# Casting v block by block, slicing W_in, and scores by tanh and pow, in a cross-covariance attention + GELU MLP kernel

One NeuronCore of one Trainium2 chip. The metric is the device time of one execution in microseconds (us), median over runs; lower is better.

## The reference

```python
def _attn_ref(q, k, v, tau):                 # each (4, 6080, 256) float32, tau = 1
    qn = q / (np.linalg.norm(q, axis=1, keepdims=True) + 1e-06)
    kn = k / (np.linalg.norm(k, axis=1, keepdims=True) + 1e-06)
    s = kn.transpose(0, 2, 1) @ qn / tau     # 256 x 256 per batch
    s = s - s.max(-1, keepdims=True)
    a = np.exp(s)
    a /= a.sum(-1, keepdims=True) + 1e-09
    return (v @ a).astype(np.float32)

# x is the attention's output, its four batches one below the other; c (line cut) is sqrt(2 / pi)
def _moe_ref(x, w_in, w_out):                # (24320, 256), (256, 2048), (2048, 256)
    h = x @ w_in
    g = 0.5 * h * (1.0 + np.tanh(c * (h + 0.044715 * h * h * h)))
    return (g @ w_out).astype(np.float32)
```

## The kernel before

Attention is folded into the first MLP product: per batch the kernel computes the Gram matrix of q and k and the sums of squares, then the scores, then `AW` = softmax times W_in. After that each block of 512 tokens (12 blocks per batch, 48 in all) takes a first product with `AW`, a gelu on ScalarE, and a second product with W_out. v must arrive transposed, so it is cast to bf16 through DRAM by a DMA from GpSimd and read back by transposing DMAs from SyncE. While one batch's blocks run, the next batch's q and k are loaded, and its Gram rows go between the block's matmuls. The parts that matter (cuts are marked by dots):

```python
qkp = ctx.enter_context(tc.tile_pool(name="qkp", bufs=6))
...
def cast_v(b, t0, t1):
    nc.gpsimd.dma_start(out=v_bf[b][t0:t1, :], in_=v[b, t0:t1, :])

def load_vt(n):                       # block n of v, transposed
    ...
    for cc in range(2):
        nc.sync.dma_start_transpose(
            out=vT[:, cc, :cols], in_=v_bf[b][t0 : t0 + cols, cc * 128 : cc * 128 + 128])
...
def scores(b):
    ss = SS[b]                        # sums of squares, the same in every partition
    nc.scalar.activation(lnk, ss[:, 256:512], AF.Ln, bias=eps)
    # ... VectorE takes q's sums off the diagonal into qq ...
    nc.scalar.activation(rk, lnk, AF.Exp, scale=-0.5)
    nc.scalar.activation(lnq, qq, AF.Ln, bias=eps)
    nc.scalar.activation(rq, lnq, AF.Exp, scale=-0.5, bias=log_it)
    # ... S = G * rk on VectorE ...
    for jc in range(2):
        nc.scalar.activation(eT[:, jc, :], S[:, jc, :], AF.Exp, scale=rq[:, jc : jc + 1])
    nc.scalar.preload_act_table(AF.Gelu_apprx_tanh)
...
        VC = 1024
        for c in range(nch):
            load_qk(0, c)
            if c == 3:
                cast_v(0, 0, VC)      # blocks 0 and 1
                load_vt(0)
            squares(0, c)             # (cut: on the last chunk a GpSimd memset of its padding)
            for i in range(len(rows_of(0, c))):
                gram_row(0, c, i)
                ss_row(0, c, i)
        nc.gpsimd.dma_start(out=win_bf, in_=moe_w_in.rearrange("(c p) d -> p c d", p=128))
        nc.gpsimd.dma_start(out=wout_bf, in_=moe_w_out.rearrange("(t p) d -> p t d", p=128))
        cast_v(0, VC, N)
        load_vt(1)
        scores(0)
        ...
        for n in range(NN + 1):       # 48 blocks; blk = n % 12, nxt = next batch
            for p in range(PAIRS):    # 8 steps
                if p == 0: load_vt(n + 2)
                mm1(n, p)             # first product and gelu
                mm2(n - 1, p)         # second product of the block before
                if p == 7: store(n - 1)
                if p == 0 and 1 <= blk <= 6: load_qk(nxt, blk - 1)
                if p == 0 and blk == 7:      cast_v(nxt, 0, N)
                # blk 2 to 7: Gram rows of chunk blk - 2 of the next batch
                # blk 8: ss_total, scores, row_sums;  blk 9: aw_part
```

## Time and profile before

| | before |
|---|---|
| median of 4 runs | 824.0 us (821.0 to 825.3) |
| span of the profiled run | 821.1 us |
| PE busy, mean granted clock | 92%, 0.969 |
| block 0's first product starts | 50.6 us |
| block 0's start to the end of block 3 | 81.55 us |
| blocks 8 to 12 (scores of batch 1) | 83.23 us |
| blocks 20 to 24 (batch 2), 32 to 36 (batch 3) | 81.76 us, 82.50 us |

"Block n" in these rows means pass n of the loop above; a pass ends where the store in it is issued, which is the output of block n - 1. The last three rows are lengths of stretches cut at those points. Between these stretches PE is 100% busy. The lines themselves are in the prediction. In them and in all lines below, PE is TensorE, DVE is VectorE, ACT is ScalarE, POOL is GpSimd and SP is SyncE; a row of a timeline has its start and length in us, and `[x <-y]` says that the engine was idle for x us before it and what ended that. A transfer has landed when all its data is in place.

### The profile page before, as it was taken

What the parts mean: (1) busy time and instruction counts of PE and PEld (TensorE: products, weight loads), DVE (VectorE), ACT (ScalarE), POOL (GpSimd) and SP (SyncE); (2) the same over time, 40 slices, a digit from 0 to 9 for tenths busy, and PEclk for the clock granted to TensorE, in tenths of its full rate; (3) what the DMA queues carried; (4) which work ended last, traced back from release to release, by engine and by line L of the source; (5) the groups of instructions that cost most, each with busy time, mean ns of one, the idle gap of its engine ahead of it and who ended that gap; (6) DMA issues with size and microseconds to landing.
All of it is one profiled execution on the core that took longest, in us unless ns stands there. A gap on an engine that the chain in (4) does not pass through costs nothing.

```text
span 821.1 us, 11523 instructions
## 1 busy us (share of the span) xinstructions
PE 756.7 (92%) x5126; PEld 505.5 (62%) x5126; DVE 177.8 (22%) x246; ACT 473.8 (58%) x470; POOL 38.4 (5%) x75
## 2 busy tenths in 40 slices
PE   5776679999799999999799999999799999999997
PEld 2434447776457667676466666767466666666666
DVE  1121115333111133433121133343121111111111
ACT  3273346566655567565765565756756555555552
POOL 4121000201000000011000000000000000000000
PEclk9998689999899999999899999999899999999999
DMA  9999971499962213199931211212112121212111
GB/s 177 181 210 206 216 153 40 91 218 128 100 151 68 46 40 78 39 207 162 201 79 39 75 40 39 77 39 39 39 38 77 40 74 40 77 40 71 44 52 49
DMA packets 87698, 77.57 MB, mean 94 GB/s; under 512 B 53584, under 2 KB 80720, under 8 KB 87120
## 3 DMA queue, kind: packets, MB, share of 16 engines
q0 software_dynamic: 10784, 39.46, 26.8%
q1 hardware_dynamic: 76864, 37.37, 20.6%
q8 instruction: 40, 0.66, 0.3%
q14 instruction: 10, 0.08, 0.0%
HBM read 78.91 MB, written 37.36 MB: 142 GB/s over the span
## 4 chain that ended last, share of the span: by engine, by line
PE 79%; DMA 16%; ACT 2%; SPq 1%; issue 0%; POOL 0%; DVE 0%; DVEq 0%; POOLq 0%
PE yp L263 37%; PE hp L243 36%; DMA vT<-vbf 9%; PE G L153 4%; DMA vbf<-in_v_dram 3%; DMA kt<-in_k_dram 2%; SPq L99 1%; DMA qt<-in_q_dram 1%; PE ps L219 1%; ACT g L247 1%; PE ss L166 0%; ACT L198 0%; ACT L189 0%; ACT L187 0%; ACT L179 0%
## 5 line engine op out<-in xcount | busy, mean ns | idle before, releaser
L247 ACT ACTIVATE g<-hp 128x1024 bf16<-128x1024 f32 (+1 forms) x384 | 388.9, 1015 | 298.5 <-PE hp L243 296.8
L243 PE MATMUL hp<-vT,aw 128*128 128x512 bf16 (+1 forms) x1536 | 398.4, 383 | 39.7 <-DMA vT<-vbf 21.4
L263 PE MATMUL yp<-wout_bf,g 128*128 128x256 bf16 (+1 forms) x3072 | 402.0, 275 | 0.0
L263 PEld LDWEIGHTS <-g 128*128 128x128 bf16 (+1 forms) x3072 | 303.3, 99 | 118.6 <-issue 7.3
L243 PEld LDWEIGHTS <-aw 128*128 128x128 bf16 x1536 | 150.6, 99 | 153.1 <-issue 44.5
L269 DVE COPY ysb<-yp 128x512 f32<-128x512 f32 x92 | 63.6, 691 | 481.2 <-PE yp L263 481.2
L153 PE MATMUL G<-kt,qt 128*128 128x256 bf16 (+1 forms) x384 | 76.6, 282 | 12.9 <-DMA kt<-in_k_dram 12.9
L120 ACT ACTIVATE sq<-qt 128x2048 bf16<-128x2048 bf16 (+3 forms) x25 | 45.0, 1801 | 26.0 <-DMA qt<-in_q_dram 13.4
L153 PEld LDWEIGHTS <-qt 128*128 128x128 bf16 (+1 forms) x384 | 38.5, 101 | 25.5 <-issue 10.2
L121 DVE TENSOR_TENSOR sq<-kt 128x2048 bf16<-128x2048 bf16 (+3 forms) x25 | 28.9, 1154 | 30.7 <-DMA kt<-in_k_dram 28.0
L166 PE MATMUL ss<-sq,ones_bf 128*128 128x512 bf16 (+1 forms) x48 | 21.0, 437 | 2.6 <-DVE sq L121 2.6
L133 DVE TENSOR_TENSOR a<-a 128x1024 f32<-128x1024 bf16 x18 | 22.0, 1225 | 0.6
L131 DVE TENSOR_TENSOR a<-sq 128x2048 bf16<-128x2048 bf16 x18 | 21.9, 1215 | 0.0
L219 PE MATMUL ps<-win_bf,eT 128*128 128x512 bf16 x64 | 19.8, 405 | 2.2 <-DMA win_bf<-in_moe_w_in_dram 2.2
L226 DVE TENSOR_SCALAR aw<-ps,rs 128x512 bf16<-128x512 f32 x16 | 12.0, 751 | 39.7 <-PE ps L219 39.7
L119 POOL MEMSET sq<- 128x512 bf16 x4 | 2.1, 525 | 383.1 <-DVE a L131 371.5
L79 POOL DMA_DIRECT2D qt<-in_q_dram x25 | 13.9, 554 | 80.6 <-ACT g L247 59.0
L224 ACT ACTIVATE aw<-ps,rs 128x512 bf16<-128x512 f32 x16 | 11.0, 688 | 7.4 <-PE ps L219 7.4
L79 POOL DMA_DIRECT2D kt<-in_k_dram x25 | 13.8, 553 | 25.2 <-DMA vbf<-in_v_dram 11.4
L142 DVE TENSOR_TENSOR acc<-acc,a 128x512 f32<-128x512 f32 x15 | 10.4, 692 | 0.5
L141 DVE TENSOR_TENSOR a<-a 128x512 f32<-128x512 f32 x15 | 10.4, 692 | 0.5
L219 PEld LDWEIGHTS <-eT 128*128 128x128 bf16 x64 | 6.5, 102 | 5.6 <-DMA win_bf<-in_moe_w_in_dram 2.3
(40 smaller groups left out, 67.4 us busy)
## 6 DMA issues: line engine op xcount, KB each, us to landing
out_dram<-ysb SPq DMA_DIRECT2D x44, 512.0 KB, 3.3
qt<-in_q_dram POOLq DMA_DIRECT2D x20, 512.0 KB, 14.5
kt<-in_k_dram POOLq DMA_DIRECT2D x20, 512.0 KB, 16.9
vbf<-in_v_dram POOLq DMA_DIRECT2D x3, 3040.0 KB, 28.8
vbf<-in_v_dram POOLq DMA_DIRECT2D x1, 2528.0 KB, 23.5
vT<-vbf SPq DMA_TRANSPOSE x96, 3.6
out_dram<-ysb SPq DMA_DIRECT2D x4, 384.0 KB, 2.6
qt<-in_q_dram POOLq DMA_DIRECT2D x3, 448.0 KB, 8.0
```

Source lines behind the costliest of these rows:

```text
L79: nc.gpsimd.dma_start(out=t[:, 0:n, :], in_=src[b, 0 : R * 128, :].rearrange("(p r) c -> p r c", r=R)[:, r0 : r0 + n, :])
L120: nc.scalar.activation(sq[:, 0:n, 0:256], qt[:, 0:n, :], AF.Square)
L121: nc.vector.tensor_mul(sq[:, 0:n, 256:512], kt[:, 0:n, :], kt[:, 0:n, :])
L131: nc.vector.tensor_add(a1, sq[:, 0:4, :], sq[:, 4:8, :])
L133: nc.vector.tensor_add(a2, a1[:, 0:2, :], a1[:, 2:4, :])
L153: nc.tensor.matmul(G[b][:, jc, :], lhsT=qt[:np_, r, jc * 128 : jc * 128 + 128], rhs=kt[:np_, r, :], start=first and jc == 0, stop=last and ...
L166: nc.tensor.matmul(SS[b], lhsT=ones_bf[:np_, :], rhs=SQ[b, c][:np_, r, :], start=first, stop=last)
L219: nc.tensor.matmul(ps, lhsT=ET[b][:, jc, ic * 128 : ic * 128 + 128], rhs=win_bf[:, jc, fs * 512 : fs * 512 + 512], start=jc == 0, stop=jc ...
L243: nc.tensor.matmul(hp[:, u, :cols], lhsT=AW[b][:, cc, fc * 128 : fc * 128 + 128], rhs=vt_tiles[n][:, cc, :cols], start=cc == 0, stop=cc == 1)
L247: nc.scalar.activation(GS[n][:, 2 * p : 2 * p + 2, :cols], hp[:, :, :cols], AF.Gelu_apprx_tanh)
L263: nc.tensor.matmul(yp[:r, s % 2, :], lhsT=GS[n][:, fc, s * 128 : s * 128 + r], rhs=wout_bf[:, fc, :], start=fc == 0, stop=fc == FC - 1)
L269: nc.vector.tensor_copy(ysb[:, s - 1 : s + 1, :], yp)
```

## The change

Three intents: (1) v is cast in pieces of 512 tokens, three blocks ahead of use, through a pool of four buffers, so that a block no longer waits for a cast of several MB; one transpose of 256 columns replaces two of 128. (2) W_in comes in four column slices right behind batch 0's q and k; batch 0's row sums run one chunk behind its Gram rows; the padding memset moves from GpSimd to VectorE. (3) Batches 1 to 3 get their scores without Ln and Exp: norms by a pow of 0.5 on GpSimd, and exp(x) as (1 + tanh(x/2)) / (1 - tanh(x/2)). One eviction of batch 0's `AW` also moves from ScalarE to VectorE (not shown).

```diff
-    dram = ctx.enter_context(tc.tile_pool(name="dram", bufs=1, space=bass.MemoryType.DRAM))
+    dram = ctx.enter_context(tc.tile_pool(name="dram", bufs=4, space=bass.MemoryType.DRAM))
...
-        sizes = [8, 8, 8, 8, 8, 4, 3] if b == 0 else [8, 8, 8, 8, 8, 7]
+        sizes = [8, 8, 8, 8, 8, 5, 2] if b == 0 else [8, 8, 8, 8, 8, 7]
...
-    def cast_v(b, t0, t1):
-        nc.gpsimd.dma_start(out=v_bf[b][t0:t1, :], in_=v[b, t0:t1, :])
+    def cast_v(n):
+        ...
+        vb = dram.tile([BLK, C], BF16, tag="vb", name=f"vb{n}")
+        nc.gpsimd.dma_start(out=vb[:cols, :], in_=v[b, t0 : t0 + cols, :])
+        v_bf[n] = vb
...
-        for cc in range(2):
-            nc.sync.dma_start_transpose(
-                out=vT[:, cc, :cols], in_=v_bf[b][t0 : t0 + cols, cc * 128 : cc * 128 + 128])
+        nc.sync.dma_start_transpose(out=vT[:, :, :cols], in_=v_bf.pop(n)[:cols, :])
...
-            nc.gpsimd.memset(sq[:, n, :], 0.0)
+            nc.vector.memset(sq[REM:, n, :], 0.0)
...
+    def norms(b):
+        ... # VectorE: q's sums off the diagonal to sv[:, 256:258], k's copied to sv[:, 0:256]
+        rt = smx.tile([128, 258], FP32, tag="rt")
+        nc.gpsimd.tensor_tensor(rt, sv, halves, op=ALU.pow)
+    def scores_a(b):
+        ... # VectorE: rt + 1e-6, reciprocal, S = G * rr
+    def scores_b(b):
+        ... # ScalarE: th = tanh(S * rh), twice
+    def scores_c(b):
+        ... # VectorE: eT = (1 + th) / (1 - th)
...
-            if c == 3:
-                cast_v(0, 0, VC)
+            if c == 1:
+                cast_v(0)
                 load_vt(0)
             squares(0, c)
             for i in range(len(rows_of(0, c))):
                 gram_row(0, c, i)
-                ss_row(0, c, i)
+            if c: ... # ss_row of chunk c - 1; those of the last chunk after the loop
-        nc.gpsimd.dma_start(out=win_bf, in_=...)
+        for fs in range(4):
+            nc.gpsimd.dma_start(out=win_bf[:, :, fs * 512 : fs * 512 + 512], in_=wi[...])
+        cast_v(1)
+        load_vt(1)
         nc.gpsimd.dma_start(out=wout_bf, in_=...)
-        cast_v(0, VC, N)
-        load_vt(1)
+        cast_v(2)
...
                         load_vt(n + 2)
+                    if p == 0 and n + 3 < NN:
+                        cast_v(n + 3)
                     mm1(n, p)
...
-                    if p == 0 and blk == ncn + 1:
-                        cast_v(nxt, 0, N)
...
                     if blk == 8:
                         if p == 2:
                             ss_total(nxt)
-                            scores(nxt)
+                            norms(nxt)
                         if p == 6:
+                            scores_a(nxt)
+                    if blk == 9:
+                        if p == 1: scores_b(nxt)
+                        if p == 2: scores_c(nxt)
+                        if p == 7:
                             row_sums(nxt)
-                    if blk == 9:
+                    if blk == 10:
                         aw_part(nxt, p // 2, p % 2, "act" if p % 2 else "dve")
```

## The prediction

> **What bounds the kernel now.** I read the page first, then the busy times by stretch, the waits of the matmul engine, the timeline around each idle gap, and the time to landing of the transposes.
>
> The page's 40 slices (20.5 us each, in tenths busy) come first.
>
> ```profile
> PE   5776679999799999999799999999799999999997
> ...
> PEclk9998689999899999999899999999899999999999
> DMA  9999971499962213199931211212112121212111
> ```
>
> The matmul row is full but for slices 0 to 5 and for single slices (10, 19, 28); the clock dips at the same places. DMA is full exactly in the early hole. So there are two kinds of loss: one where transfers are the bound, and three short ones, one per later batch. Stretches cut at the output stores show them (columns: stretch, length, busy us and instructions of each engine, granted clock, DMA share, GB/s).
>
> ```profile
> 0.00:50.60 50.60, 30.34 (x156) 16.63 (x157) 10.50 (x21) 17.40 (x17) 16.01 (x33) 0.93 1.01 181
> 50.60:132.15 81.55, 60.75 (x365) 37.29 (x364) 15.10 (x19) 37.77 (x37) 4.80 (x9) 0.85 0.89 176
> 132.15:194.71 62.56, 62.56 (x449) 43.57 (x448) 25.06 (x29) 39.60 (x37) 5.85 (x11) 1.00 0.70 135
> 194.71:218.20 23.49, 17.58 (x106) 10.73 (x105) 2.73 (x9) 16.89 (x19) 2.66 (x5) 0.85 1.47 85
> ...
> 385.82:409.33 23.51, 17.60 (x106) 10.68 (x105) 2.73 (x9) 16.88 (x19) 2.67 (x5) 0.85 1.11 205
> 409.33:575.46 166.13, 166.13 (x1168) 113.78 (x1167) 46.87 (x57) 102.23 (x99) 0.53 (x1) 1.00 0.22 53
> 575.46:599.71 24.25, 18.34 (x106) 11.01 (x105) 2.72 (x9) 16.88 (x19) 0.00 (x0) 0.86 0.12 33
> ```
>
> Where PE is 100% busy nothing can be won: 62.56 us are four token blocks with Gram work, 15.64 us each, and the plain block takes 13.9 us (spacing of the last stores). A pair of steps (4 matmuls of 512 columns, 8 of 256) starts every 1.74 us, 2.35 columns per ns. The losses are in the rest.
>
> Early hole, waits of PE from 40 to 135 us, and PE in it:
>
> ```profile
> PE hp L243 <- DMA vT<-vbf: 20.4, 3, 9.3
> ...
> 79.38 0.61 PE L243 MATMUL hp<-vT,aw 128*128 128x512 bf16 x1 [5.27 <-DMA vT<-vbf]
> 89.33 1.44 PE L243 MATMUL hp<-vT,aw 128*128 128x512 bf16 x3 [9.34 <-DMA vT<-vbf]
> 113.52 1.44 PE L243 MATMUL hp<-vT,aw 128*128 128x512 bf16 x3 [5.75 <-DMA vT<-vbf]
> ```
>
> Blocks 2 and 3 wait for the transposed v. The transposes were late twice over: the 5 MB cast of v landed at 64.5 us, and behind it next batch's q and k filled the queue. Time to landing of a transpose, first in 60 to 120 us, then after 260 us:
>
> ```profile
> DMA to landing us min/median/max: 3.3/18.9/37.8
> ...
> DMA to landing us min/median/max: 2.6/3.4/24.6
> ```
>
> Scores hole, ACT from 390 us:
>
> ```profile
> 390.91 1.28 ACT L179 ACT_TABLE_LOAD   x1
> 392.20 0.47 ACT L179 ACTIVATE lnk<-ss,eps 128x256 f32<-128x256 f32 x1
> 392.70 1.28 ACT L187 ACT_TABLE_LOAD   x1
> ...
> 398.58 1.28 ACT L198 ACT_TABLE_LOAD   x1
> ```
>
> Five loads of 1.28 us lie between two gelus (390.89 to 399.87); PE then shows a 5.91 us gap and four matmuls taking 1.86 in place of 1.03 us.
>
> **What the Trainium skill says.** "ScalarE: Activation LUTs", section What ACT_TABLE_LOAD costs, gives about 1283 ns for a load plus about 1380 ns of drain. The trace agrees on the load (1.28 us, five of them), but shows no drain of that length beside it: 8.98 us are 6.4 us of loads, 2.4 us of activations (0.47, 0.42, 0.29, 0.29 and 0.91) and small gaps. "TensorE: Matmul & The Clock Gate", Part 1, says that an idle window of about 3.4 us halves the clock; the trace agrees (granted clock 0.85 over each scores block, that is half speed for some 7 of 23.5 us). "DMA: Bandwidth & Descriptors", Queues, rings and completion order, says each engine alternates between queues packet by packet, so a transpose beside a full software queue waits for a load packet at each turn; 18.9 against 3.4 us fits. "GPSIMD Engine Reference", section 3.1, gives some 2.6 cycles per element for a two-input add and nothing for pow; no row of this trace has GpSimd arithmetic of that form, so pow is the term I cannot size.
>
> **Part 1: the start, up to the first gelu block.** Now: the last k part is in at about 37.7 us (issued 24.39, 13.3 us to landing); the last chunk's squares wait for PE to free a buffer until 38.6; sums end at 42.1; scores of batch 0 end at 44.8; then PE waits 2.2 us for W_in, whose issue sat 11.58 us behind a GpSimd memset, to 39.14; block 0 starts at 50.6. The change moves the memset to DVE, so W_in queues straight behind k, and its first slice (512 KB read, about 1.2 us at the 428 GB/s of reads that 214 GB/s written in bf16 means) is in by 40 us: that wait goes. 512 rows fewer of v go ahead of k: 1.2 us. Gram rows no longer queue behind sums that need squares, and the 3.6 us gap at 28.7 us, with the half clock after it, should shrink: another 1 to 2 us. Sum: block 0 starts at about 46, 4.6 us earlier.
>
> **Part 2: the early hole.** Ideal from block 0 on is 10.3 us (block 0 now, paced by its gelus) + 13.9 + 2 x 15.64 = 55.5 us up to the end of block 3; now it is 132.15 - 50.6 = 81.55 us. So 26.0 us are waits and half-clock restarts. In the new kernel v comes in 256 KB pieces (bf16), and each cast must wait until an older buffer has been transposed; q and k of the next batch are queued between the casts, so the queue can't run 10 MB ahead. What stays: behind k come W_in (1 MB), v block 1, W_out (1 MB), v blocks 2, 3 and 4, and one q/k chunk (1 MB): 4.2 MB or 19.6 us at 214 GB/s from about 36.5 us, so to 56 us, with transposes beside it to 59. Block 1 needs its v at 46 + 10.3 = 56.3 us, its cast lands at about 45, and its transposes share the queue with this backlog. I charge a stall of 2.5 us with the restart. Block 2's v (needed at 70 us) has the queue mostly to itself. Gain: 23.5 us.
>
> **Part 3: scores of batches 1 to 3.** The scores blocks take 23.49, 23.51 and 24.25 us. Without the hole such a block is 13.9 + 0.86 (two fp32 matmuls, 390.54 to 391.40) + 0.2 (last Gram row) = 15.0 us, so 8.5 + 8.5 + 9.2 = 26.2 us are lost. New on ACT: two tanh of 128x256 at about 0.46 us, 0.9 us; a gelu takes 1.02 of each 1.74 us and two PSUM buffers cover the slip, so nothing on the path if no table is loaded. New on DVE: some 5 us over ten steps of 1.74 us, on an engine 22% busy. New on GpSimd: one pow of 128x258. From the sums (end of step 2) to tanh (step 1 of the next block) are seven steps, 12.2 us; DVE work ahead and behind takes about 3.5 us. A pow up to about 9 us is hidden. I charge 1 us for all three. Gain: 25.2 us. The W_in product for the next batch moves a block later, at the same cost.
>
> **Part 4: the rest.** Batch 1's v in one 3 MB cast delayed one block at 236 us by 1.1 us and made that block 15.82 instead of 14.33 us: 1.5 us gained. The tail is untouched.
>
> **Sum.** 4.6 + 23.5 + 25.2 + 1.5 = 54.8 us; 822.8 - 54.8 = 768. Check from below: of the 90 us that PE's span has over its columns (1.72 million at 2.35 per ns, 731 us), the first load, block 0's gelus and the last store remain.
>
> **Rivals.** (a) Pow is slow. For: GpSimd is the slowest for such work, and DVE waits in order behind it, with output evictions queued after. Against: someone left four steps between norms and their use, as if it had been measured. At 20 us some 11 us per batch come back: 800. (b) The transpose wait stays: HWDGE still meets a full software queue in 45 to 60 us, and GpSimd in program order holds q and k back behind a cast that waits for a buffer. For: 18.9 us median beside loads. Against: blocks 1 and 2 have two blocks' lead, after which there is 1.25 MB (6 us of queue) per 15.6 us block. A full transpose delay at blocks 1 and 2 gives 778. (c) Part 1 is worth nothing, because k lands no earlier with transposes of block 0 now beside it: 773. (d) All hidden, no stall at block 1: 762.
>
> **Range and chances.** Parts 2 and 3 are holes seen in the trace, removed at the cause; both would have to fail to stay within 2% (above 806). (d) gives the low end, (b) with (c) or a pow of some 13 us the high end: 757 to 785. Faster 0.96, same 0.03, slower 0.01.
>
> **What would show it.** No wait of PE on the transposes in 60 to 135 us, and block 3 ending near 104 us (Part 2); block 0's first gelu near 46 us (Part 1); no table load after about 45 us, scores blocks of about 15 us, full clock there (Part 3). DVE waiting on pow for over 3 us, or PE on gelu near each batch's eighth block, would prove rival (a); PE waiting on transposed v at blocks 1 to 3, rival (b). The prediction is wrong if pow takes over 12 us, if tanh makes a table load, or if the single transpose of 256 columns is much slower than the two of 128.

## The result, and the profile after

The changed kernel takes **913.4 us** (4 runs, 912.2 to 914.6) against 824.0 us. The ratio is 1.1091 (95% interval 1.1053 to 1.1128): slower by 11%, where I had said 768 us and faster. A ratio here is the mean time of one kernel's fast runs over that of the other's fast runs of the same rounds, so it is not quite the ratio of the medians quoted.

The page's slices (22.8 us each, tenths busy), to be laid beside those of before:

```profile
PE   4657999992388999999147899999905999999997
...
POOL 3412000039720000004962000000595000000000
PEclk9988999997598999999669899999966999999999
DMA  9999521210599121211069913122107321212201
```

The early hole is still there (slices 2 and 3, counted from 0), and each single-slice hole of before is now two to three slices wide. POOL, nearly idle before, is full in or just ahead of each. DMA has a peak right after each POOL peak. One group explains POOL:

```profile
L217 POOL TENSOR_TENSOR rt<-sv,halves 128x258 f32<-128x258 f32 x3 | 125.0, 41653 | 395.3 <-DVE sv L215 395.3
```

The pow takes 41.65 us each time. The chain of waits hands it on; here are VectorE, ScalarE and PE behind the first one, each from its own timeline:

```profile
237.92 0.29 DVE L223 TENSOR_SCALAR rt<-rt 128x258 f32<-128x258 f32 x1 [40.20 <-POOL rt L217]
```

```profile
240.58 0.91 ACT L236 ACTIVATE th<-S,rh 128x256 f32<-128x256 f32 x2 [32.98 <-DVE S L229]
```

```profile
242.44 1.86 PE L292 MATMUL hp<-vT,aw 128*128 128x512 bf16 x4 [31.56 <-ACT g L296]
277.79 1.67 PE L292 MATMUL hp<-vT,aw 128*128 128x448 bf16 x4 [8.57 <-DMA vT<-vb]
```

VectorE waits 40.2 us for pow, ScalarE's tanh 33.0 us for VectorE, and PE 31.6 us for the gelu queued behind the tanh. A second gap follows 35 us later, on transposed v. What lies between is the GpSimd queue (start, length, instruction, idle before it):

```profile
87.31 0.49 POOL L93 DMA_DIRECT2D vb<-in_v_dram  x1 [2.39 <-DMA qt<-in_q_dram]
196.22 41.66 POOL L217 TENSOR_TENSOR rt<-sv,halves 128x258 f32<-128x258 f32 x1 [108.42 <-DVE sv L215]
237.86 2.48 POOL L93 DMA_DIRECT2D vb<-in_v_dram  x5
240.33 0.56 POOL L79 DMA_DIRECT2D qt<-in_q_dram  x1
```

For 108 us GpSimd issues nothing, because the pow at the head of its queue waits for its input; then it computes 41.7 us; then everything queued behind goes out at once.

The waits of PE over the whole run, and the stretches (before: 83.23, 81.76 and 82.50 us for the three with scores):

```profile
PE hp L292 <- ACT g L296: 94.9, 4, 31.6
PE hp L292 <- DMA vT<-vb: 36.4, 4, 13.8
```

```profile
49.20:126.95 77.75, 58.73 (x365) 36.76 (x364) 15.05 (x19) 37.62 (x37) 8.96 (x17) 0.89 0.77 141
126.95:189.51 62.56, 62.56 (x449) 43.58 (x448) 25.41 (x30) 39.61 (x37) 0.00 (x0) 1.00 0.19 51
189.51:307.34 117.83, 77.70 (x504) 50.09 (x503) 17.77 (x29) 43.53 (x46) 55.30 (x27) 0.84 0.54 113
...
415.23:532.96 117.73, 77.16 (x504) 49.90 (x503) 17.77 (x29) 43.53 (x46) 55.28 (x27) 0.84 0.54 113
...
640.85:747.92 107.07, 75.52 (x504) 49.41 (x503) 17.77 (x29) 43.53 (x46) 47.75 (x13) 0.86 0.30 66
```

The books close. Block 0 starts 1.4 us earlier (49.2), blocks 0 to 3 take 3.8 us less, the three scores stretches take 34.6, 36.0 and 24.6 us more: together +90.0 us, and the spans differ by 911.2 - 821.1 = 90.1 us. Batch 3 is cheaper by 10.7 us than batches 1 and 2: there is no batch 4 whose q and k could come in a burst. (That the burst is the reason is shown by e5 and e8 below.)

### The profile page after: what moved, and what is told of

The parts are those of the page before. It is cut to its first block, busy times and chain, and to the rows that moved or that the text cites. A ratio compares the mean times of both kernels' runs of the same rounds, so it can differ in the third digit from the quotient of the medians.

```text
span 911.2 us, 11507 instructions
## 1 busy us (share of the span) xinstructions
PE 756.7 (83%) x5126; PEld 506.4 (56%) x5126; DVE 200.3 (22%) x273; ACT 448.9 (49%) x442; POOL 185.4 (20%) x120
## 4 chain that ended last, share of the span: by engine, by line
PE 66%; DMA 17%; POOL 14%; DVE 1%; ACT 1%; issue 0%; DVEq 0%; POOLq 0%
PE yp L312 32%; PE hp L292 30%; POOL rt L217 14%; DMA vT<-vb 12%; DMA qt<-in_q_dram 4%; PE G L156 3%; DMA wout_bf<-in_moe_w_out_dram 2%; DVE rr L224 1%; PE ps L268 0%; ACT th L236 0%; PE ss L174 0%; ACT g L296 0%; POOL qt L79 0%; POOL kt L79 0%; DVE sv L215 0%
## 5 line engine op out<-in xcount | busy, mean ns | idle before, releaser
L217 POOL TENSOR_TENSOR rt<-sv,halves 128x258 f32<-128x258 f32 x3 | 125.0, 41653 | 395.3 <-DVE sv L215 395.3
L156 PE MATMUL G<-kt,qt 128*128 128x256 bf16 (+1 forms) x384 | 71.6, 290 | 16.1 <-DMA kt<-in_k_dram 16.1
L236 ACT ACTIVATE th<-S,rh 128x256 f32<-128x256 f32 x6 | 2.7, 500 | 98.9 <-DVE S L229 98.9
L93 POOL DMA_DIRECT2D vb<-in_v_dram x48 | 24.4, 511 | 33.4 <-DMA qt<-in_q_dram 26.2
L169 PE MATMUL ss<-sq,ones_bf 128*128 128x512 bf16 (+1 forms) x48 | 11.7, 386 | 0.0
```

Source lines behind the costliest of these rows:

```text
L93: nc.gpsimd.dma_start(out=vb[:cols, :], in_=v[b, t0 : t0 + cols, :])
L156: nc.tensor.matmul(G[b][:, jc, :], lhsT=qt[:np_, r, jc * 128 : jc * 128 + 128], rhs=kt[:np_, r, :], start=first and jc == 0, stop=last and ...
L217: nc.gpsimd.tensor_tensor(rt, sv, halves, op=ALU.pow)
```

## The experiments

Twelve kernels ran, in three sets of four; all gave correct results. "Before" is the old kernel, run in the same rounds (medians 821.6, 822.4 and 821.8 us). My theory A was: pow's duration, plus a burst of loads queued behind it, is the whole loss.

### e1: the change with the old scores

```diff
-                            norms(nxt)          # and scores_a, _b, _c; aw_part in block 10
+                            scores(nxt)         # aw_part in block 9
```

> The changed kernel with the old scores (Ln, Exp, table loads) for batches 1 to 3; everything else of the change stays. Theory A (the pow of 41.65 us on GpSimd, and the loads queued behind it, are the whole loss): 816 to 819 us, since the changed kernel's block 3 ended 5.2 us earlier than before (126.95 against 132.15) and the second v wait of the old kernel goes (1.5 us). Rival B (the casts of v by block, the W_in slices or the single transpose cost time after block 3 too): above 830 us.

Measured 817.6 us (ratio 0.9982, 0.9921 to 1.0042). Theory A holds and rival B falls: everything but the scores is no slower than before, and no faster worth naming. So the loss is in part 3, and parts 1 and 2 had gained next to nothing.

### e2: the kernel before with the new scores only

```diff
-                            scores(nxt)
+                            norms(nxt)          # and scores_a, _b, _c; aw_part in block 10
```

> The kernel before with nothing but the new scores (pow, tanh) put in. Theory A: slower by three times 33.9 less 8.5 us (stall and half clock with pow, less the old table loads), +76 us, so 899 us, and up to 20 us more if the loads that wait behind the pow collide with transposes as in the changed kernel. Rival B: well below 870 us.

Measured 919.2 us (ratio 1.1205, 1.1162 to 1.1248), within the bounds of A, at its upper end: pow again takes 41.64 us three times, PE stalls 31.6 us behind each, and after batches 1 and 2 there are waits on transposed v of 4.6 and 3.9, and 4.3 and 1.9 us. The loss is the new scores', whichever way v is cast.

### e3: e1 with a pow that nobody reads

```diff
                             scores(nxt)
+                            unused_pow(nxt)     # GpSimd; 258, 129, 4 columns in batches 1, 2, 3
```

> The kernel of the first run with a pow on GpSimd beside the old scores whose result nobody reads: 258 columns for batch 1, 129 for batch 2, 4 for batch 3. Theory A, if pow's time goes by columns: 41.7, 20.8 and 0.7 us. What it costs the whole shows how much of the loss comes from the loads that GpSimd can't issue meanwhile: theory A has 10.7 us for batch 1 and as much or less for batch 2 (one burst of loads beside the transposes each), none for batch 3, so 10 to 21 us over the first run. Rival C (the blocked issue is the main loss, not the wait of VectorE and ScalarE for the result): over 35 us.

Measured 852.9 us (ratio 1.0409), 35.3 us over e1.

```profile
L255 POOL TENSOR_TENSOR rt<-sv,halves x3: 1032/21036/41654, 198.6 to 615.6; 128x258 f32<-128x258 f32 x1, 128x129 f32<-128x129 f32 x1, 128x4 f32<-128x4 f32 x1
```

Pow goes by columns: (41.65 - 1.03) / 254 = 0.160 us for each column of 128 partitions, and some 0.4 us fixed (21.0 us for 129 columns by this, 21.04 measured). My estimate of what blocking the queue costs (10 to 21 us) was too low: PE now waits on transposed v for 15.1 and 3.7 us in batch 1 and 9.9 us in batch 2, each with a restart at half clock. Rival C's sign (over 35 us) is met, if barely: a blocked GpSimd queue alone is dear, with no one waiting for pow's result. In the changed kernel most of this should be hidden, since PE stands still anyway while pow runs; that is an argument, and e8 shows how the two losses share out there.

### e4: pow on 4 columns

Both norms are taken off the diagonal (2 columns of q, 2 of k), and PE spreads k's inverse norms over the partitions by multiplying a matrix of ones with a diagonal matrix, into the sums' own PSUM tile.

```diff
-        nc.gpsimd.tensor_tensor(rt, sv, halves, op=ALU.pow)              # 128x258
+        nc.gpsimd.tensor_tensor(rt, sv, halves[:, 0:4], op=ALU.pow)      # 128x4
...
+        nc.tensor.matmul(SS[b][:, 0:256], lhsT=ones_f, rhs=dk, start=True, stop=True)
```

> The changed kernel with pow on 4 columns (both norms taken off the diagonal, k's spread to all partitions by a product of the matrix of ones with a diagonal matrix) in place of 258. Theory A: no stall of PE on gelu at the scores, but the loads of the next batch still wait behind the pow until block 8 and then come in one burst, so 790 to 812 us; with pow at a fixed cost of many us whatever its size, above 830. Without the burst it would be 789 or less (824 less 5.2, 1.5, 26.2 and 2).

Measured 808.2 us (ratio 0.9843, 0.9808 to 0.9878), within A's range. No wait of PE on gelu over 0.2 us is left. Pow takes 1.03 us, and yet a wait on transposed v stays behind each of batches 1 and 2:

```profile
241.55 1.67 PE L301 MATMUL hp<-vT,aw 128*128 128x448 bf16 x4 [5.20 <-DMA vT<-vb]
```

e1, without pow, has no such wait after block 3: there, q and k of batch 2 go out one chunk per block, as the Gram rows of batch 1 free their buffers. A pow in the same queue, even this short one, holds those loads back until block 8, when all six chunks' buffers are free. GpSimd in e1, and then in e4:

```profile
112.40 0.56 POOL L79 DMA_DIRECT2D qt<-in_q_dram  x1 [13.12 <-PE G L156]
...
128.02 0.55 POOL L79 DMA_DIRECT2D qt<-in_q_dram  x1 [14.02 <-ACT g L296]
```

```profile
196.94 1.04 POOL L216 TENSOR_TENSOR rt<-sv,halves 128x4 f32<-128x4 f32 x1 [108.25 <-DVE junk L212]
```

In e4 all six chunks of batch 2 follow that pow, from 200.4 to 233.8 us.

### e5 to e7: pacing the loads, and block 1 of v early

e5 is e4 with one tiny GpSimd copy per block that reads the block's first gelu result; GpSimd's loads for that block come after it in its queue. For this the cast moves from before `mm1` to behind it.

```diff
                     mm1(n, p)
+                    if p == 0:
+                        nc.gpsimd.tensor_copy(pj, GS[n][0:1, 0, 0:1])
                     if p == 0 and n + 3 < NN:
                         cast_v(n + 3)
```

> The kernel with pow on 4 columns, plus one tiny GpSimd copy per block that reads the block's first gelu result, ahead of the block's cast of v and q/k loads: GpSimd can no longer issue loads of later blocks early. Theory A (the waits on transposed v that are left, 12.1, 8.0, 5.2 and 5.6 us, all come from transposes that share the DMA engines with a burst of GpSimd's loads): all four waits go with their half-clock restarts, 766 to 774 us, and transposes land in under 10 us. Rival D (the transposes are late because their own cast lands late, or because one transpose of 256 columns is slow by itself): the waits at blocks 1 and 2 stay, over 785 us.

e6 is e4 with block 1's v handled in the Gram phase; e7 has both edits.

```diff
                 cast_v(0)
                 load_vt(0)
+                cast_v(1)
+                load_vt(1)
```

> The kernel with pow on 4 columns, with block 1 of v cast and transposed in the Gram phase, as the kernel before did, and no pacing. Theory A: the wait at block 1 goes, but the burst is still there, so that the wait moves to blocks 2 and 3, and little is won: 798 to 808 us. Rival D (the late cast of block 1 is the cause): 14 us or more are won, below 795 us.

> Both of the two edits before. Theory A: as the paced kernel, within 3 us (764 to 774 us), since with no burst block 1's transpose is in time either way.

| | time, us | ratio to before (95%) |
|---|---|---|
| e5 paced | 769.9 | 0.9364 (0.9338 to 0.9389) |
| e6 early | 794.0 | 0.9660 (0.9633 to 0.9687) |
| e7 both | 771.4 | 0.9379 (0.9353 to 0.9406) |

The paced kernel loses all four waits. Its page:

```profile
PE   3689999999999999999999999999999999999997
...
PEclk9999999999999999999999999999999999999999
DMA  8995775552235657632422766553224226234111
...
PE 94%; DMA 4%; ACT 0%; DVE 0%; POOL 0%; issue 0%; DVEq 0%; POOLq 0%
```

Time to landing of a transpose, first in the changed kernel from 40 to 100 us, then in e5 from 40 to 130 us:

```profile
DMA to landing us min/median/max: 11.2/29.8/38.4
```

```profile
DMA to landing us min/median/max: 3.3/3.7/9.5
```

Same transposes, same casts, same bytes: 29.8 us beside the burst, 3.7 without. In e5 block 1's cast has the same place in the queue as in e4 and the transpose is the same single one, so neither a late cast nor the single transpose is the cause by itself, and rival D falls. e6 missed my range by 4 us, and its time is where rival D had put it (below 795 us, 14 us won): I had thought the wait would only move from block 1 to block 2. The landings show why it did not. Beside the burst the transposes land late and one after another (in the changed kernel at 72.2, 93.2 and 99.1 us for blocks 1, 2 and 3); with block 1's done before the burst, block 2's lands at 78.0 us in place of 93.9 (e4). So a late block 1 is part of the loss only while the burst is there. Doing it early moves all of them up, and 14 us are won; the burst still costs 5.9, 6.3 and 5.6 us of waits. With pacing there is nothing left for it to win (e7).

### e8: e7 with the change's own pow

```diff
-        nc.gpsimd.tensor_tensor(rt, sv, halves[:, 0:4], op=ALU.pow)      # and the diagonals
+        nc.gpsimd.tensor_tensor(rt, sv, halves, op=ALU.pow)              # 128x258
```

> The kernel of the third run with the change's own pow on 258 columns back. With no burst left, what remains of pow is the wait of VectorE and ScalarE for it: theory A has three times 33.9 us (31.6 of stall and 2.3 at half clock, from batch 3 of the changed kernel) over the third run: 866 to 877 us. Rival C (the blocked issue is the main loss): under 845.

Measured 870.1 us (ratio 1.0591), 98.7 us over e7, and no wait on transposed v at all: rival C falls for the changed kernel, and 32.9 us per batch is what waiting for this pow costs alone, against the one on 4 columns. The burst adds 10.7 us in each of batches 1 and 2 of the changed kernel, on top of that. With the early hole this accounts for all that lies between the changed kernel and e7 (913.4 - 771.4 = 142.0 us): 98.7 for the pow, 21.4 for the two bursts, and 21.8 between block 0's start and the end of block 3, a stretch of 77.75 us in the changed kernel and 56.0 in the paced e5.

### f1 to f4: what the other parts are worth

All four start from e5 or its counterpart, and ran together.

```diff
f4: e1 with e5's pacing (old scores, no pow)
f1: e5 with W_in in one transfer:          nc.gpsimd.dma_start(out=win_bf, in_=wi)
f2: e5 with ss_row(0, c, i) beside gram_row(0, c, i), as before
f3: e5 with two transposes of 128 columns per block, as before
```

> The paced kernel with the old scores (Ln, Exp and table loads) for batches 1 to 3, no pow at all. If the table loads cost what the trace of before showed, 8.2 us per batch (5.9 of stall, 2.3 at half clock), this is 24.6 us over the paced kernel with pow on 4 columns: 793 to 797 us.

> The paced kernel with W_in in one transfer in place of four slices. The four slices had all landed by 42.4 us, before the product that reads them could start (46.2 us), so the slices should be worth nothing: 768 to 772 us. If they are worth the 2.2 us that the kernel before waited for W_in: 772 us or more, with a wait of PE on W_in.

> The paced kernel with batch 0's row sums beside its Gram rows, as before, and not one chunk behind. In the paced kernel the last k part lands at 37.3 us and the sums end at 43.2, since three groups of sums come after the last Gram rows and the buffers of the squares come free late. Theory: the old order is as good or better here, 766 to 770 us; if the new order was worth the 1 to 2 us that I predicted, 771 us or more.

> The paced kernel with two transposes of 128 columns per block in place of one of 256. With no burst to share the engines with, both land in time, so the same time within 2 us: 768 to 772 us.

| | time, us | ratio to before (95%) |
|---|---|---|
| f4 old scores | 792.0 | 0.9644 (0.9609 to 0.9679) |
| f1 W_in in one | 769.5 | 0.9373 (0.9336 to 0.9409) |
| f2 sums beside Gram | 766.5 | 0.9331 (0.9301 to 0.9362) |
| f3 two transposes | 773.0 | 0.9412 (0.9377 to 0.9448) |

f4 against e5: the scores without table loads are worth about 22 to 23 us over three batches (792.0 - 769.9, and the difference of the ratios, 0.028 of 822), a little under my 24.6. f4 against e1: pacing alone is worth some 26 us. f1: the W_in slices are worth nothing here, since W_in in one transfer lands at 42.0 us and its first use is at 44.3. f3 is 1 us above my range. Its interval overlaps those of f1 and e5 (0.9364, other rounds), but its four runs (771.2 to 775.2) all lie above f1's four of the same rounds (768.3 to 770.5), and its trace has two waits of PE on k (1.3 and 1.4 us) that f1's lacks; the single transpose may be worth some 3 us, which these runs suggest and don't settle. f2 is the fastest kernel: its four runs (765.8 to 766.9) all lie below f1's, by 3.0 us in the mean, and its block 0 starts at 45.3 us where f1's starts at 47.7 and e5's at 49.2.

One cheaper change was not tried. Batch 0's scores run the same Ln and Exp with no table load between them (42.18 to 44.79 us in the trace of before) and one after, because the program loads the set `natural_log_exp_and_others` beforehand; batches 1 to 3 load five times. Loading that set ahead there too would spare three of five loads, by estimate 3.85 us per batch, with no pow and no tanh.

The last Gram and sum rows of e5 (first) and f2 (second):

```profile
38.70 1.89 PE L169 MATMUL ss<-sq,ones_bf 128*128 128x512 bf16 x8
40.42 0.92 PE L156 MATMUL G<-kt,qt 128*128 128x256 bf16 x6
41.28 2.00 PE L169 MATMUL ss<-sq,ones_bf 128*128 128x512 bf16 x8
```

```profile
39.33 0.39 PE L156 MATMUL G<-kt,qt 64*128 64x256 bf16 x2
39.56 0.38 PE L169 MATMUL ss<-sq,ones_bf 64*128 64x512 bf16 x1
```

With the sums a chunk behind, 16 sum rows and 3 Gram rows are still to do after 38.7 us, although the last of k had landed at 37.3; side by side they end 3.3 us sooner.

## Why the prediction was wrong

**Reading the old kernel was right.** The two kinds of hole are real, and with both removed at the cause the kernel runs in 769.9 us (e5), or 766.5 (f2), where I had predicted 768. That the sums agree to 2 us is partly luck, since e5's block 0 starts only 1.4 us earlier (I had 4.6) and its early hole gives 25.6 us (81.55 less 56.0; I had 23.5). One line was read too narrowly: the DMA row is full not "exactly in the early hole" but also in slices 8 to 10 and 17 to 19, where PE is mostly busy. But the change as written removed neither hole, and I had credited it with both.

**Part 3, the step "A pow up to about 9 us is hidden. I charge 1 us for all three."** The window was about right (41.65 less 32.9 is 8.8 us); the size of pow was not. It measured 41.65 us, so 32.9 us per batch of waiting (e8) in place of 0.3, some 99 us in all. I named pow as the one term I could not size, as rival (a), and still gave slower a chance of 0.01. Even the 20 us that I set in the rival makes 800 us, outside my range; the page's add rate gave no upper bound for pow, and the argument that someone had spaced the steps "as if it had been measured" was no evidence. The rest of Part 3 held: tanh needed no table load (none ran after 45.7 us), it cost 0.5 us each, and dropping the loads is worth 7.7 us per batch (a third of 23.0 us, f4 against e5 by ratios) against the 8.4 that I credited.

**Part 2, the step "each cast must wait until an older buffer has been transposed".** It doesn't. The pool's `bufs=4` rotates nothing in DRAM: in the built program's instruction list (place in GpSimd's list, line, output<-input; not a trace) each cast writes a tensor of its own, and its only waits are for an earlier load's completion:

```
30 L93 DMACopy vb_324<-in_v_dram 16x8192 [waits DMASW5_49]
32 L93 DMACopy vb_329<-in_v_dram 16x8192 [waits DMASW7_49]
37 L93 DMACopy vb_573<-in_v_dram 16x8192 [waits DMASW4_49]
```

The trace agrees: block 5's cast was issued at 43.05 us, while block 1's transpose, whose buffer it would have had to reuse, landed at 72.2. What held GpSimd back was eight loads in flight: the load issued at 54.82 us had waited 9.7 us for W_out, the eighth load before it. With six chunk buffers free it sent all of batch 1's q and k by 83 us, as before. So "the queue can't run 10 MB ahead" failed, and rival (b) took its place: 13.8 us of wait at block 1 (I charged 2.5) and 5.0 at block 2. Block 1 was even worse off than before, where it had been transposed in the Gram phase. The gain was 3.8 us where I had 23.5. Pacing, which I had believed to be in the change, is worth that much when it is put in (about 26 us, f4 against e1).

**Part 2 again, an effect that I did not see.** Without pow (e1) the next-but-one batch's loads go out one chunk per block while Gram rows free their buffers. A pow in the same in-order queue ends that, and the loads come in one burst at the moment when transposes are needed. That is 10.7 us each for batches 1 and 2 of the changed kernel; it is shown by e4, whose pow of 1 us still leaves waits of 5.2 and 5.6 us, and by e5, which removes them.

**Part 1, "4.6 us earlier".** It was 1.4 us in the profiled run; other traces with the sums a chunk behind have block 0 at 47.2 to 50.3 us. The W_in wait did go, but the term "another 1 to 2 us" for running sums a chunk behind had the wrong sign: it costs some 3 us (f2 against f1 and e5). With the old order the block starts about where I had put it (45.3, I had 46).

**Part 4 (1.5 us).** The wait that it counted, 1.1 us at 236 us, is gone, but the burst put one of 8.6 us a little later (277.8 us).

## What to carry to other kernels

In this kernel GpSimd issues the casting loads, in the order of its program. A pow of 1.03 us put among them, which waits for data from late in the loop, turned steady loads into a burst (e4): so look at what an instruction waits for, and not only at its length, before putting it in front of loads. Here pacing the loads by what consumes them worked (e5, f4) and counting on buffers did not. Before trusting that a rotating pool throttles a transfer, look in the instruction list or in the trace for the wait that would do it. And a term that cannot be sized from any row belongs in the range, not in a charge of 1 us: run that one instruction first.

## What the Trainium skill lacked or had wrong

- "GPSIMD Engine Reference", section 3.1, has about 2.6 cycles per element for a two-input add, which would be an estimated 0.56 us for 258 columns at its 1.2 GHz; it has nothing on pow, which measured 41.65 us for 128x258, 21.04 for 128x129 and 1.03 for 128x4, so 0.160 us per column, some 75 times the add's estimate for 258.
- "DMA: Bandwidth & Descriptors", Rules for kernel authors, says that a transpose next to ordinary DMAs "needs nothing". That row is about correctness; in time, transposes of one block landed in 29.8 us (median) beside a full GpSimd load queue and in 3.7 us beside paced loads. No page gives this factor.
- No page says what it costs when loads from GpSimd stand in line behind a compute instruction that waits: here 108 us without an issue, then a burst, and two waits of PE of 5.2 and 5.6 us with a pow of only 1.03 us.
- "ScalarE: Activation LUTs", What ACT_TABLE_LOAD costs, has a load at about 1283 ns, which the trace confirms to the ns, plus about 1380 ns of drain at each switch, of which nothing shows: in the trace of before the load began 0.02 us after the gelu ahead of it ended (390.89), and the activation after the load 0.01 us after its end (390.91 + 1.28 against 392.20).
- The same page's list of table sets does not say which set tanh shares with the tanh gelu; six tanh ran between gelus here with no load.
